# Unequal halves for the products of the values in a two-layer linear-attention kernel

## The chip, the cores and the metric

The kernel runs on one core of a Trainium2 chip, as one program. The metric is the time of the device in microseconds (us), the median of several runs. One further run was taken with the hardware profiler; what is said of single engines comes from that one.

## What is computed

A stack of four residual blocks on 2048 rows of 640 numbers: attention, a dense block, then the same two again with the same weights. Cut to what matters here:

```python
qkv = (x @ wqkv).reshape(B, S, 3, H, Dh)            # H = 32 heads of Dh = 20
q, k, v = qkv[0], qkv[1], qkv[2]                    # after a transpose, per head
phi_q = concat([softmax(q @ w_phi), softmax(-(q @ w_phi))])
phi_k = concat([softmax(k @ w_phi), softmax(-(k @ w_phi))])
kv = einsum("bhsf,bhsd->bhfd", phi_k, v)
z = phi_k.sum(axis=s)
o = (phi_q @ kv) / (phi_q @ z + 1e-6)
x = x + o.reshape(B, S, D) @ wo                     # D = 640; x is normed before
x = x + mish(norm(x) @ w1 + b1) @ w2                # F = 1536
```

The change concerns `v`: for every row, 640 sums of products (32 heads times 20) from a normed row of 640.

## The kernel before

The 2048 rows are 16 tiles of 128, taken two by two in 8 blocks. Per layer there are three parts: `attend_first` makes queries, keys and values of each tile and adds up `kv` and `z` over all tiles; `attend_second` turns them into the attention's output; `dense` is the dense block. Each part runs over the 8 blocks. Both layers do the same, so that values are made for 32 tiles in all.

**Split numbers.** Every product with weights is done three times in the reduced-precision format `F32R`, on high and low parts (`h` and `l`): high rows with high weights, high with low, low with high. `project_half` (L352 to L359) does this for the values, the keys, the queries and the output projection: for each of five chunks k of 128 input columns it issues three TensorE products, so 15 for one half of the output columns. All have the line L358 in the profile. The stationary operand of each is a 128x128 piece of the rows (`xth` or `xtl`), which is loaded anew by a weight load before each product (PEld in the profile); the moving operand is a piece of the weights, `w` columns wide. `project` (L343) calls it for both halves. For the values `w` is HC = 320, for keys and queries FC = 304 (19 differences per head).

**Values.** `values` (L448) makes one tile: a column of ones, 30 products of 320 columns in two halves, and a copy by ScalarE out of PSUM into the tile `v`, where each head has 21 columns. In the first block of a layer (i < BT, 2 tiles) the halves go to two one-bank PSUM tiles `one` and are copied one by one; in the other blocks (14 tiles per layer) they go to the two banks of one tile `mm`, and one instruction copies all 640 columns. There are two `mm` buffers, which keys, queries, values and the output projection share.

**Order.** For TensorE, VectorE and GpSimd a scheduler decides the order when the program is built. ScalarE's copies and activations go through the helper `act` (L116; in the profile they all have the line L122), which ties each to the one before, so that they keep the order of the code. `keys` and `queries` are generators that are taken on step by step; their features (`features`, L374) are a copy out of `mm`, reductions and differences on VectorE, an exponential on ScalarE, a sum and a quotient, and for queries a transpose and a store to `e_d`. Each block works its tiles in an order of its own, in most of them k0, v0, q0, k1, v1, q1. The product of keys and values (L432) reads the finished `v`. A query's tile `r` is one of two buffers, and ScalarE's first write to it waits until the store of the tile before last has left.

Of the kernel before, what the change touches and what calls it, by code (L numbers as in the profile page):

```python
# [10 lines left out]
AF = mybir.ActivationFunctionType  # L11
# [7 lines left out]
D = 640  # L19
F = 1536  # L20
H = 32
DH = 20
KD = D // P
KF = F // P
BT = 2
# [4 lines left out]
HC = D // 2  # L30
# [18 lines left out]
def kernel(  # L49
# [22 lines left out]
    def mm_tile():  # L72
        return psum.tile([P, 2, 512], F32, tag="mm", name="mm", bufs=2)

    def one_tile():
        return psum.tile([P, 512], F32, tag="one", name="one", bufs=4)
# [39 lines left out]
    def act(*args, **kw):  # L116

        if last_act[0] is None:
            ins = nc.scalar.activation(*args, **kw)
        else:  # L120
            with tc.issue_after(last_act[0]):
                ins = nc.scalar.activation(*args, **kw)  # L122
        last_act[0] = ins.ins
# [49 lines left out]
    def load_v_weights():  # L173

        ws = [r1_pair(k) for k in range(KD)]
        for k in range(KD):
            split(ws[k][0][:, D:2 * D], ws[k][1][:, D:2 * D], wv[k * P:(k + 1) * P, :],
                  (row_tile, row_tile, v_tile, v_tile, big_tile)[k])
        return ws
# [163 lines left out]
    def project(xts, t, ws, col, ps=None, w=HC):  # L343

        if ps is None:
            mm = mm_tile()
            ps = [mm[:, 0], mm[:, 1], mm]
        for c in range(2):
            project_half(ps[c], xts, t, ws, col, c, w=w)
        return ps  # L350

    def project_half(ps, xts, t, ws, col, c, ks=range(KD), w=HC):  # L352
        sl = slice(t * P, (t + 1) * P)
        cs = slice(col + c * w, col + (c + 1) * w)
        for k in ks:
            h, l, wh, wl = xts.hs[k], xts.ls[k], ws[k][0][:, cs], ws[k][1][:, cs]
            for n, (a, r) in enumerate(((h, wh), (h, wl), (l, wh))):
                nc.tensor.matmul(ps[:, :w], a[:, sl], r, start=(k == 0 and n == 0),  # L358
                                 stop=(k == KD - 1 and n == 2))  # L359

    def both(ps, w=HC):

        return ps[2][:, :, :w]
# [43 lines left out]
    def attend_first(layer, x_src, first):  # L407
# [40 lines left out]
        def values(xts, i, v):  # L448
            vv = v.rearrange("p (h d) -> p h d", d=DH + 1)
            act(vv[:, :, DH], ident[:, :H], AF.Copy, scale=0.0, bias=1.0)  # L450
            if i < BT:
                pv = project(xts, i, kv_ws, D, [one_tile(), one_tile()])
                for c in range(2):
                    act(vv[:, c * H // 2:(c + 1) * H // 2, :DH],
                        pv[c][:, :HC].rearrange("p (h d) -> p h d", d=DH), AF.Copy)
            else:
                pv = project(xts, i % BT, kv_ws, D)
                act(vv[:, :, :DH].rearrange("p (c h) d -> p c h d", c=2),
                    both(pv).rearrange("p c (h d) -> p c h d", d=DH), AF.Copy)
            yield  # L460

        if first is None:
            with tc.manual_schedule(engines={mybir.EngineType.SP}):
# [11 lines left out]
                kv_ws = load_v_weights()  # L475
# [3 lines left out]
        else:  # L479
            nxt, kv_ws = first  # L480
            q_ws = load_q_weights()
        for b in range(NB):
            xts = nxt
# [8 lines left out]
            for n, (kind, t) in enumerate(order):  # L492
                t = int(t)
                i = b * BT + t
                if b == 0 and n == 1:
                    if layer:
                        load_k_weights(kv_ws)
                if b == 0 and n == 3:
                    if layer == 0:
                        fold_phi(kv_ws, bd, raw)  # L500
                    kva = one_tile()
                if b == NB - 1 and n == 3:
                    loaded = {0: load(0)}
                if b + 1 < NB:
                    if n == 0:
                        xt = fetch_normed(b + 1)
                    elif n == 2:
                        nxt = xt if layer else normed(b + 1, xt)
                    elif n > 2:
                        nxt.step()  # L510
                g = {"k": lambda: keys(xts, i, vs[t]), "q": lambda: queries(xts, i),
                     "v": lambda: values(xts, i, vs[t])}[kind]()
                next(g)
                advance()
                pending.append(g)
# [388 lines left out]
```

## Time and profile before

| what | us |
|---|---|
| median of 3 runs (lowest to highest) | 1399.29 (1398.11 to 1399.91) |
| the profiled execution's own time | 1397.5 |
| its span in the profile | 1395.7 |
| TensorE busy | 1364.8 |
| weight loads busy | 1344.2 |
| VectorE busy | 1080.8 |
| ScalarE busy | 592.4 |
| GpSimd busy | 466.4 |

The span reaches from the first to the last instruction; the 1.8 us that the time has beyond it lie around the program. PE is TensorE's matmul, PEld its weight load, DVE is VectorE, ACT ScalarE, POOL GpSimd. A matmul's duration in the profile is its latency, and the next starts long before it ends: what a product costs in a stream is the distance from one start to the next, which the timeline shows. Each matmul has its own weight load.

### The profile page before, as it was taken

The numbers are of one execution on the slowest core, as the hardware profiler recorded it, in microseconds if no ns is written. First come the engines' busy times: TensorE is split into PE (matmuls) and PEld (weight loads), VectorE is DVE, ScalarE is ACT, GpSimd is POOL, SyncE is SP. The second block draws the span as 40 slices with busy tenths as digits, with TensorE's granted clock in tenths as the row PEclk, the third lists the DMA queues.
The fourth block names the chain that finished last, engine by engine and source line by source line (L and its number), as shares of the span: only waits on it lengthen the run. The fifth ranks groups of instructions, "written<-read, shape, count | busy, mean of one in ns | idle before, by whom it ended". The sixth has DMA issues, their size and how long they took to land. (4 is left out here: it accounts for less than half of the span.)

```text
span 1395.7 us, 30855 instructions
## 1 busy us (share of the span) xinstructions
PE 1364.8 (98%) x12866; PEld 1344.2 (96%) x12866; DVE 1080.8 (77%) x1814; ACT 592.4 (42%) x1039; POOL 466.4 (33%) x346
## 2 busy tenths in 40 slices
PE   7999999999999999999999999999999999999998
PEld 7989999899999999999999999999999999999998
DVE  5798888686688877788759988878667766777775
ACT  4444443321355454454454334332134544444443
POOL 1454544243442221222234454543344211211112
PEclk9999999999999999999999999999999999999999
DMA  8533423779534433444374333358965212333200
GB/s 312 166 60 77 75 41 70 204 224 317 194 89 95 100 82 60 102 114 95 103 258 85 78 72 70 58 126 253 273 246 172 76 29 68 95 96 95 59 37 20
DMA packets 350277, 169.03 MB, mean 121 GB/s; under 512 B 287097, under 2 KB 323689, under 8 KB 350137
## 3 DMA queue, kind: packets, MB, share of 16 engines
q1 hardware_dynamic: 350137, 167.06, 44.4%
q8 instruction: 101, 1.65, 0.5%
q14 instruction: 39, 0.32, 0.1%
HBM read 104.43 MB, written 62.59 MB: 120 GB/s over the span
## 5 line engine op out<-in xcount | busy, mean ns | idle before, releaser
L745 PE MATMUL mm<-r2h,ol 128*128 128x320 f32 x1280 | 305.3, 310 | 1.4 <-ACT ol L728 0.8
L729 POOL TENSOR_TENSOR ol<-big,ol 128x512 fp32r<-128x512 f32 (+1 forms) x98 | 130.1, 1329 | 456.2 <-ACT ol L728 390.9
L703 PE MATMUL one<-xtl,r1h 128*128 128x256 f32 x960 | 268.6, 280 | 2.0 <-DVE xtl L300 2.0
L703 PE MATMUL one<-xth,r1l 128*128 128x256 f32 x960 | 268.0, 279 | 0.0
L703 PE MATMUL one<-xth,r1h 128*128 128x256 f32 x960 | 266.5, 279 | 0.0
L745 PEld LDWEIGHTS mm<-r2h,ol 128*128 128x128 f32 x1280 | 219.1, 188 | 2.7 <-POOL ol L729 1.5
L745 PE MATMUL mm<-r2l,ol 128*128 128x320 f32 x640 | 197.3, 309 | 0.0
L358 PE MATMUL mm<-r1h,xth 128*128 128x304 f32 (+1 forms) x600 | 187.5, 313 | 6.6 <-ACT r L122 6.6
L358 PE MATMUL mm<-r1h,xtl 128*128 128x304 f32 (+1 forms) x600 | 184.7, 308 | 1.0 <-DVE xtl L300 1.0
L358 PE MATMUL mm<-r1l,xth 128*128 128x304 f32 (+1 forms) x600 | 184.4, 307 | 0.0
L703 PEld LDWEIGHTS one<-xtl,r1h 128*128 128x128 f32 x960 | 180.4, 188 | 2.7 <-DVE xtl L300 2.5
L703 PEld LDWEIGHTS one<-xth,r1l 128*128 128x128 f32 x960 | 180.4, 188 | 0.0
L703 PEld LDWEIGHTS one<-xth,r1h 128*128 128x128 f32 x960 | 179.9, 188 | 0.0
L718 DVE TENSOR_SCALAR big<-big 128x512 f32<-128x512 f32 (+1 forms) x98 | 55.9, 571 | 113.6 <-ACT big L716 113.5
L358 PE MATMUL mm<-r2h,xth 128*128 128x304 f32 (+1 forms) x460 | 142.2, 309 | 0.0
L358 PE MATMUL mm<-r2h,xtl 128*128 128x304 f32 (+1 forms) x460 | 140.4, 305 | 0.0
L358 PE MATMUL mm<-r2l,xth 128*128 128x304 f32 (+1 forms) x460 | 140.3, 305 | 0.0
L716 ACT ACTIVATE big<-one,b1s 128x256 f32<-128x256 f32 x192 | 80.8, 469 | 96.2 <-PE one L703 95.6
L358 PEld LDWEIGHTS mm<-r1h,xth 128*128 128x128 f32 x600 | 113.8, 190 | 8.1 <-ACT r L122 7.0
L720 ACT ACTIVATE big<-big,two 128x512 f32<-128x512 f32 (+1 forms) x98 | 70.3, 717 | 118.8 <-DVE big L719 116.2
L745 PEld LDWEIGHTS mm<-r2l,ol 128*128 128x128 f32 x640 | 120.2, 188 | 0.0
L399 POOL TENSOR_TENSOR r<-r,r 128x1280 f32<-128x1280 f32 x32 | 77.0, 2406 | 124.1 <-DVE r L398 108.7
(131 smaller groups left out, 3031.9 us busy)
## 6 DMA issues: line engine op xcount, KB each, us to landing
e_d<-r SPq DMA_DIRECT2D x128, 160.0 KB, 4.0
big<-e_d SPq DMA_DIRECT2D x32, 640.0 KB, 5.9
x_d<-xt SPq DMA_DIRECT2D x23, 640.0 KB, 3.9
xt<-x_d SPq DMA_DIRECT2D x22, 640.0 KB, 4.6
n_d<-xn SPq DMA_DIRECT2D x176, 80.0 KB, 2.3
xt<-in_x SPq DMA_DIRECT2D x16, 640.0 KB, 5.5
xn<-x_d SPq DMA_DIRECT2D x28, 320.0 KB, 4.1
v<-n_d SPq DMA_DIRECT2D x30, 256.0 KB, 3.1
```

The lines of the kernel that those rows point to most:

```text
L358: nc.tensor.matmul(ps[:, :w], a[:, sl], r, start=(k == 0 and n == 0), stop=(k == KD - 1 and n == 2))
L399: nc.gpsimd.tensor_tensor(eg, eg, r.unsqueeze(2).to_broadcast([P, 2 * H, DH]), op=ALU.mult)
L703: nc.tensor.matmul(ph[:, j, :], l, r, start=(n == 0), stop=(n == 3 * KD - 1))
L716: exps[0] = nc.scalar.activation(part(ta, 0)[:, j - js.start], ph[:, j, :], AF.Exp, bias=b1s[:, 2 * pr + j:2 * pr + j + 1]).ins
L718: nc.vector.tensor_scalar_min(e, e, E_CAP)
L720: nc.scalar.activation(r, n, AF.Ln, bias=two)
L729: nc.gpsimd.tensor_tensor(al[:, js], n, ah[:, js].bitcast(F32), op=ALU.subtract)
L745: nc.tensor.matmul(pys[t][:, c, :HC], l[:, j, sl], r, start=(f == 0 and n == 0), stop=(f == KF - 1 and n == 2))
```

## The change

The halves of the values become 24 heads (480 columns) and 8 heads (160 columns). The 24 heads go to the first PSUM bank, the 8 to the second. Each part is copied by an instruction of its own, in all blocks, and the first copy stands in ScalarE's order ahead of the second. The number of products and of weight loads stays: 15 of 480 and 15 of 160 columns in place of 30 of 320.

```diff
             if i < BT:
-                pv = project(xts, i, kv_ws, D, [one_tile(), one_tile()])
-                for c in range(2):
-                    act(vv[:, c * H // 2:(c + 1) * H // 2, :DH],
-                        pv[c][:, :HC].rearrange("p (h d) -> p h d", d=DH), AF.Copy)
+                pv = [one_tile(), one_tile()]
             else:
-                pv = project(xts, i % BT, kv_ws, D)
-                act(vv[:, :, :DH].rearrange("p (c h) d -> p c h d", c=2),
-                    both(pv).rearrange("p c (h d) -> p c h d", d=DH), AF.Copy)
+                mm = mm_tile()
+                pv = [mm[:, 0], mm[:, 1]]
+            for c, (h0, h1) in enumerate(((0, 24), (24, H))):
+                n = (h1 - h0) * DH
+                project_half(pv[c], xts, i % BT, kv_ws, D + h0 * DH - c * n, c, w=n)
+                act(vv[:, h0:h1, :DH], pv[c][:, :n].rearrange("p (h d) -> p h d", d=DH), AF.Copy)
             yield
```

`project_half` takes the columns from `col + c * w`; for c = 1 the argument `D + 480 - 160` makes that D + 480.

## The prediction

> **What bounds the kernel now.** I read the page's first part for the busiest engine, then the busy time of stretches that hold the values (75 to 255 us and, in the second layer, 740 to 935 us), then TensorE's waits, and then the groups of products by shape and the timeline for what one product costs. The first part and four of the stretches:
>
> ```profile
> PE 1364.8 (98%) x12866; PEld 1344.2 (96%) x12866; DVE 1080.8 (77%) x1814; ACT 592.4 (42%) x1039; POOL 466.4 (33%) x346
> ```
>
> ```profile
> 75.00:100.00 25.00, 21.52 (x256) 20.58 (x256) 24.97 (x31) 9.07 (x15) 15.44 (x9) 0.93 0.28 53
> ...
> 150.00:200.00 50.00, 50.00 (x562) 49.22 (x549) 43.84 (x57) 22.59 (x38) 26.52 (x15) 1.00 0.32 58
> ...
> 740.00:780.00 40.00, 35.84 (x414) 34.79 (x413) 39.56 (x40) 14.82 (x25) 20.46 (x10) 0.96 0.33 71
> ...
> 830.00:880.00 50.00, 50.00 (x568) 49.22 (x554) 43.44 (x49) 19.88 (x34) 25.23 (x12) 1.00 0.38 71
> ```
>
> The columns are length, PE, PEld, DVE, ACT, POOL, TensorE's granted clock and the DMA. TensorE works 98% of the span and every microsecond of the steady stretches, at clock 1.00. Only early in each layer has it gaps (3.5 us before 100, 4.2 us before 780), and there VectorE is full. The waits say what for:
>
> ```profile
> PE mm L358 <- ACT r L122: 6.6, 2, 3.5
> ```
>
> That is one stall per layer (3.5 and 3.1 us): both `mm` buffers are taken, and ScalarE's copy of a query comes late. Outside of these, time added to TensorE's stream is time added to the end.
>
> **What one product costs.** The products of the values, 960 in all (840 into `mm`, 120 into `one`):
>
> ```profile
> L358 PE MATMUL mm<-r1h,xth 128*128 128x320 f32 x280 | 88.2, 315 | 3.1 <-ACT r L122 3.1
> L358 PE MATMUL mm<-r1h,xtl 128*128 128x320 f32 x280 | 87.2, 311 | 0.0
> L358 PE MATMUL mm<-r1l,xth 128*128 128x320 f32 x280 | 87.1, 311 | 0.0
> ...
> L358 PE MATMUL one<-r1h,xtl 128*128 128x320 f32 x40 | 12.3, 309 | 0.0
> L358 PE MATMUL one<-r1l,xth 128*128 128x320 f32 x40 | 12.3, 309 | 0.0
> ...
> L358 PE MATMUL one<-r1h,xth 128*128 128x320 f32 x40 | 11.5, 312 | 0.0
> ```
>
> A duration of 0.31 us is latency. The distance of starts is read from the timeline, first and last row of an unbroken run, for three widths:
>
> ```profile
> 199.83 0.31 PE L358 MATMUL mm<-r1h,xtl 128*128 128x320 f32 x1
> ...
> 202.03 0.31 PE L358 MATMUL mm<-r1h,xtl 128*128 128x320 f32 x1
> ...
> 202.53 0.30 PE L358 MATMUL mm<-r2l,xth 128*128 128x304 f32 x1
> ...
> 206.45 0.30 PE L358 MATMUL mm<-r2h,xtl 128*128 128x304 f32 x1
> ```
>
> ```profile
> 385.83 0.28 PE L703 MATMUL one<-xth,r1h 128*128 128x256 f32 x1
> ...
> 390.03 0.28 PE L703 MATMUL one<-xth,r1h 128*128 128x256 f32 x1
> ```
>
> 320 columns: 15 steps in 2.20 us, 0.1467 each. 304 columns: 28 steps in 3.92 us, 0.1400. 256 columns: 36 steps in 4.20 us, 0.1167. From 304 to 320 a column costs 0.42 ns (0.0067/16), from 256 to 320 it costs 0.47 (0.0300/64).
>
> **480 columns** aren't in the trace. By the nearer slope: 0.1467 + 160 x 0.00042 = 0.2133 us; by the wider: 0.1467 + 160 x 0.00047 = 0.2217. I take 0.2133, since the rows next to it give it.
>
> **160 columns** aren't in the trace in this format. If cost followed the columns down by the same 0.42 ns, it would be 0.0800, and the pair would cost what two halves cost: nothing gained, nothing lost. What speaks against that is the weight load, one per product, 128 columns wide whatever the moving operand is. Two views: the loads after a pause, and the narrow products of L250 (float32, two instructions per product).
>
> ```profile
> 164.45 0.19 PEld L358 LDWEIGHTS mm<-r1h,xth 128*128 128x128 f32 x1
> 164.56 0.19 PEld L358 LDWEIGHTS mm<-r1l,xth 128*128 128x128 f32 x1
> 164.71 0.19 PEld L358 LDWEIGHTS mm<-r1h,xtl 128*128 128x128 f32 x1
> ```
>
> ```profile
> 38.73 1.28 PE L250 MATMUL one<-big,raw 120*128 120x114 f32 x10
> 39.94 0.41 PE L250 MATMUL one<-big,r 40*128 40x38 f32 x2
> ```
>
> ```profile
> L250 PE MATMUL one<-big,raw x17: 275/275/365, 37.7 to 40.7; 120*128 120x114 f32 x17
> ...
> L250 PE MATMUL one<-big,r x4: 277/288/298, 39.9 to 41.0; 40*128 40x38 f32 x4
> ```
>
> The second load follows the first by 0.11 us, when the queue has room; the third comes 0.15 later, as a product must first start. So loads hardly follow closer than 0.11, and one load at a time runs ahead. Ten products of 114 columns stand (1.28 - 0.275)/9 = 0.1117 us apart, and two of 38 columns 0.41 - 0.288 = 0.12: a third of the columns and not a nanosecond less. That is a floor, set by loads of 128 columns. I take 0.112 for 160 columns (nearest below in width, 114); the ends are 0.11 (the loads) and 0.1167 (256 columns, which 160 can't exceed by width).
>
> The Trainium skill ("TensorE: Matmul & The Clock Gate", LDWEIGHTS) puts a load at its columns over 1.2, which is 107 ns for 128, and the sum would then be 13.0 us in place of the 15.4 below. The same page (Back-to-back issue gap) has streams of load and product at about 81 ns for 128 columns and 131 for 512, which by a straight line between them makes 480 and 160 together as dear as twice 320: no change. The trace has 0.1117 for 114 columns and 0.1467 for 320, so that it speaks for the first.
>
> **The sum.** 480 pairs (32 tiles x 15). A pair before: 2 x 0.1467 = 0.2933. After: 0.2133 + 0.112 = 0.3253. Difference 0.032, times 480: **+15.4 us**. Ends: 480 x (0.2133 + 0.11 - 0.2933) = 14.4, and 480 x (0.2217 + 0.1167 - 0.2933) = 21.6.
>
> **The copies.** ScalarE's rows, and what it waits for ahead of writing `v`:
>
> ```profile
> L122 ACT ACTIVATE v<-mm 128x640 f32<-128x640 f32 x28 | 19.8, 707 | 78.8 <-PE mm L358 78.8
> ...
> L122 ACT ACTIVATE v<-one 128x320 f32<-128x320 f32 x8 | 3.2, 432 | 4.9 <-PE one L358 4.9
> ```
>
> A column costs (707 - 432)/320 = 0.86 ns, so 480 columns take 570 ns and 160 take 295: 865 in place of 707 in 28 tiles, 4.4 us more on an engine that is busy 42%; in the other four nothing changes (2 x 432 = 864). TensorE's stream hides it.
>
> **A new wait.** The order of the changed program shows that in those 28 tiles the first 160-column product waits for ScalarE's copy of the 480 columns, as both lie in one tile `mm`; before, the second half followed at once. The scheduler put other work between: 22 to 25 products of the next query in most tiles, 22 x 0.140 = 3.1 us, and 1.6 us in the shortest (the last block of the second layer). The copy needs 0.57 us. Is ScalarE there in time? Before the 28 copies it idled 78.8 us, 2.8 per tile, until both halves were done, 30 x 0.1467 = 4.4 us after the start. The first part is done at 15 x 0.2133 = 3.2, 1.2 us sooner, so ScalarE has 1.6 us in hand and the cover another 2.5. I cost the wait at nothing; without the cover it would be 0.57 us in each of 28 tiles, 16 us.
>
> Behind the second copy ScalarE now stands still until the 160 columns are done, and the exponential of the query before is queued there. One half block of before:
>
> ```profile
> 159.21 0.71 ACT L122 ACTIVATE v<-mm 128x640 f32<-128x640 f32 x1 [3.56 <-PE mm L358]
> 159.82 1.26 ACT L122 ACTIVATE r<-r 128x1280 f32<-128x1280 f32 x1
> ...
> 163.41 0.68 ACT L122 ACTIVATE r<-mm 128x608 f32<-128x608 f32 x1 [0.55 <-PE mm L358]
> ...
> 168.97 0.69 ACT L122 ACTIVATE big<-mm 128x608 f32<-128x608 f32 x1 [3.07 <-PE mm L358]
> ```
>
> Counted from the end of the keys (154.8), the exponential starts at 5.0 now. In the new order the keys' second half and the 480 columns are interleaved; then come 0.21 us of 480 columns, 22 products (3.1) and 15 x 0.112 = 1.7, so the copy of the 160 starts at about 5.2 (latency counted) and the exponential at 5.5. The query's copy starts at 8.6 now and at 8.65 then, since the same work of TensorE lies ahead of it. Both `mm` buffers come free in time: the values' at 5.5 (needed at 7.3, after 8 products and L432), the query's at 9.3 (needed at about 12). So the half blocks stay bound by TensorE and become 0.48 us longer each.
>
> **At the two stalls** TensorE waits for a chain on ScalarE, VectorE and DMA that doesn't get longer. Up to 3.5 tiles of values come before each, 1.7 us per layer that can vanish in it; but the new order leaves one group of 160 columns (15 x 0.112 = 1.7) for after the stall in the first layer. I take 1 us off for both layers (bounds: 3.4 off, and 1.7 on per layer).
>
> Sum: +15.4 - 1 = +14.4. On the profiled execution, 1397.5 + 14.4 = 1411.9; the median of the runs lies 1.8 above that execution, so **1413.7 us**.
>
> **The rivals.**
> 1. *No floor* (the other side): the load of a narrow product hides under the wide ones, the distance falls to 0.080, and the time stays at 1399, within 2 us either way; where the shorter last copy (295 for 707 ns) also frees `mm` early enough, it eats from the two stalls (6.6 us) and the kernel gets a little faster. It decides as soon as a load can stand more than one product ahead. The 0.12 of 38 columns speaks against it, and the Back-to-back gap that the Trainium skill states speaks for it.
> 2. *The new wait shows.* If ScalarE comes to the first copy more than 2.5 us after the 480 columns are done, TensorE stands before the 160 with the rest of the query and the next keys queued behind. One exponential late (1.26 us) would cost about 1 us in each of 28 tiles: 1413.7 + 28 = 1442. For it: ScalarE does wait for VectorE and stores early in each layer. Against it: 2.8 us of idle time per tile.
> 3. *160 columns cost what float32 costs.* No product under 256 columns in this format is in the trace. The float32 products of L250 need two instructions each, 2 x 0.1117 for 114 columns, and by columns 0.314 for 160: 480 x (0.2133 + 0.314 - 0.2933) = +112, 1511 us. Nothing in the trace asks for it; it is the upper end of what is unknown.
>
> That the change doesn't do what it says is out: the order has 480 products of each width, and the same loads.
>
> **How the numbers follow.** Forecast 0.72, rival 1 0.08, rival 2 0.12, rival 3 0.06, others 0.02. The forecast's own bounds are 1399.3 + 14.4 - 3.4 = 1410 and 1399.3 + 21.6 + 3.4 = 1424. For 8 in 10 the range must take in most of rival 2 where it shows in part of the tiles, up to 1432, and a forecast some us lower where the narrow products gain a little on the floor, 1405. A run of this kernel tells about 0.2% (2.8 us) from no change. Slower takes the forecast, rivals 2 and 3 and half of the others: 0.91; rival 1 splits into 0.06 the same and 0.03 faster.
>
> **What would show it.** In the changed profile's timeline the 160-column products would stand 0.11 us apart and the 480-column ones 0.213; TensorE stays at 50.00 of 50.00 in the steady stretches; the waits name no copy of `v` for more than a microsecond or two in all; the half blocks are 0.5 us longer. Wrong I am if the 160s stand 0.08 apart (rival 1), 0.2 or more (rival 3), or if TensorE's gaps grow with ScalarE's copy of `v` as their end (rival 2).

## The result and the profile after

The changed kernel takes 1434.63 us (median of 4 runs, 1434.15 to 1436.97), the kernel before beside it 1399.60 (1398.11 to 1402.36): a ratio of 1.0257, 95% interval 1.0238 to 1.0276. That is 35 us slower, where 14 were forecast. The profiled execution has a span of 1432.6 us, 36.9 more than before.

First the products. The changed kernel's timeline, from the second to the last product of one group of each width:

```profile
146.71 0.38 PE L358 MATMUL mm<-r1l,xth 128*128 128x480 f32 x1
...
149.56 0.38 PE L358 MATMUL mm<-r1h,xtl 128*128 128x480 f32 x1
...
153.29 0.28 PE L358 MATMUL mm<-r1l,xth 128*128 128x160 f32 x1
...
154.75 0.27 PE L358 MATMUL mm<-r1h,xtl 128*128 128x160 f32 x1
```

13 steps each: 480 columns cost 2.85/13 = 0.219 us, 160 columns 1.46/13 = 0.112. So the floor is there, at the price that was forecast; the wide product costs 0.219 in place of 0.2133. A pair is 0.038 us dearer than before, 18 us for 480 pairs. That leaves half of the loss.

Then the first part of the page and the stretches of the changed kernel (length, PE, PEld, DVE, ACT, POOL, clock, DMA):

```profile
PE 1387.7 (97%) x12866; PEld 1348.8 (94%) x12866; DVE 1088.0 (76%) x1814; ACT 592.4 (41%) x1067; POOL 463.1 (32%) x346
```

```profile
150.00:200.00 50.00, 48.89 (x508) 46.09 (x507) 42.45 (x60) 17.96 (x34) 25.28 (x16) 1.00 0.34 61
...
830.00:880.00 50.00, 47.35 (x495) 44.81 (x495) 40.27 (x44) 17.21 (x32) 19.38 (x10) 1.00 0.33 62
```

TensorE, full there before, now has gaps of 1.1 and 2.7 us in 50. ScalarE's busy time is as before (592.4). TensorE's waits:

```profile
PE one L432 <- POOL big L399: 12.8, 4, 5.5
PE mm L358 <- ACT r L122: 11.3, 6, 4.3
...
PE mm L358 <- ACT big L122: 2.8, 5, 0.6
```

The first and the last row are new, and the middle one was 6.6 with two cases. In return a wait at the end of the first part is gone that the kernel before had:

```profile
PE one L564 <- DVE xn L558: 5.3, 2, 2.7
```

By these rows the waits have grown by 12.8 + 4.7 + 2.8 - 5.3 = 15 us. With the 18 of the products that is 33 of the 36.9. A wait also costs more than its row says, 0.34 us in the case taken apart in the last section; for 11 waits more that would be about 4, an estimate from that one case.

No row names a copy of `v`: TensorE never waits long for the copy that the change puts between its two groups. It waits for a product of GpSimd that follows an exponential, for the copy of a query, and for the copy of the keys. The first two come behind the copies of `v` in ScalarE's order; the keys' copy comes ahead of them. The waits of ScalarE show where the first two were held:

```profile
ACT v L122 <- PE mm L358: 150.5, 45, 4.6
```

Before `v` it now idles 150.5 us, where it was 78.8. One half block of the changed kernel:

```profile
164.30 0.68 ACT L122 ACTIVATE big<-mm 128x608 f32<-128x608 f32 x1 [5.50 <-PE mm L358]
164.87 0.26 ACT L122 ACTIVATE v<-ident 128x32 f32<-128x32 f32 x1
164.99 0.57 ACT L122 ACTIVATE v<-mm 128x480 f32<-128x480 f32 x1
170.04 0.30 ACT L122 ACTIVATE v<-mm 128x160 f32<-128x160 f32 x1 [4.48 <-PE mm L358]
170.24 1.26 ACT L122 ACTIVATE r<-r 128x1280 f32<-128x1280 f32 x1
```

After the copy of the 480 columns ScalarE stands still for 4.48 us, until TensorE has done 22 query products and the 160 columns, and only then comes to the exponential. Here that passes. It does not pass in two places. One is the end of the first part of the attention, where too few query products are left to fill the time. The chain of what ended last, around 272 us:

```profile
268.32 4.59 PE mm L358 x36
...
272.94 0.02 ACT v L122
...
273.14 1.27 ACT big L122
...
274.43 1.49 DVE r L397
...
276.78 1.28 POOL r L389
```

and GpSimd's rows there:

```profile
276.78 1.27 POOL L389 TENSOR_TENSOR r<-r,m 128x640 f32<-128x640 f32 x1 [3.85 <-DVE m L388]
278.01 2.35 POOL L399 TENSOR_TENSOR big<-big,r 128x1280 f32<-128x1280 f32 x1
```

The exponential of the last keys stands behind the copy of the last 160 columns. It runs at 273.14, the sum on VectorE at 274.43, and GpSimd's product, in order behind the query's difference, ends at 280.4. TensorE's product of keys and values waits for it 5.5 us. In the kernel before, 45 query products stood between the last values and that product (254.28 to 260.44), and the same exponential ran at their start:

```profile
254.47 0.71 ACT L122 ACTIVATE v<-mm 128x640 f32<-128x640 f32 x1 [3.34 <-PE mm L358]
255.08 1.26 ACT L122 ACTIVATE big<-big 128x1280 f32<-128x1280 f32 x1
```

The other place is the second layer. There the exponential of a query, held in the same way, leaves VectorE idle for 2.90 us; later ScalarE stands still until the store of an earlier query has left, so that its copy of the next query comes late and TensorE waits for it:

```profile
835.82 1.49 DVE L397 TENSOR_REDUCE r<-r 128x64 f32<-128x1280 f32 x1 [2.90 <-ACT r L122]
...
854.45 0.26 ACT L122 ACTIVATE r<-ident 128x32 f32<-128x32 f32 x1 [3.66 <-DMA e_d<-r]
854.59 0.66 ACT L122 ACTIVATE r<-mm 128x608 f32<-128x608 f32 x1
...
855.30 0.49 PE L358 MATMUL mm<-r1h,xth 128*128 128x480 f32 x1 [2.65 <-ACT r L122]
```

The kernel before has no wait of TensorE for a query's copy after 760 us.

### The profile page after: what moved, and what is told of

Read it like the earlier page. It is cut to its first block, busy times and chain, and to the rows that moved or that the text cites. A ratio compares the mean times of both kernels' runs of the same rounds, so it can differ in the third digit from the quotient of the medians.

```text
span 1432.6 us, 30914 instructions
## 1 busy us (share of the span) xinstructions
PE 1387.7 (97%) x12866; PEld 1348.8 (94%) x12866; DVE 1088.0 (76%) x1814; ACT 592.4 (41%) x1067; POOL 463.1 (32%) x346
## 4 chain that ended last, share of the span: by engine, by line
PE 75%; DVE 11%; DMA 3%; issue 2%; ACT 2%; SPq 1%; POOL 0%; DVEq 0%; ACTq 0%; POOLq 0%
PE one L703 22%; PE mm L745 21%; PE mm L358 20%; PE one L358 6%; PE mm L594 3%; DMA e_d<-r 2%; DVE m L388 2%; DVE r L397 2%; PE one L294 2%; DVE xtl L300 1%; SPq L444 1%; PE one L432 1%; DVE r L440 1%; DVE big L718 1%; DVE r L391 1%
## 5 line engine op out<-in xcount | busy, mean ns | idle before, releaser
L358 PE MATMUL mm<-r1h,xth 128*128 128x304 f32 (+2 forms) x600 | 192.4, 321 | 11.3 <-ACT r L122 11.3
L358 PE MATMUL mm<-r1l,xth 128*128 128x304 f32 (+2 forms) x600 | 189.6, 316 | 0.0
L358 PE MATMUL mm<-r1h,xtl 128*128 128x304 f32 (+2 forms) x600 | 188.8, 317 | 0.0
L358 PE MATMUL mm<-r2h,xth 128*128 128x304 f32 (+1 forms) x460 | 143.0, 311 | 2.8 <-ACT big L122 2.8
L358 PE MATMUL mm<-r2l,xth 128*128 128x304 f32 (+1 forms) x460 | 140.9, 306 | 0.0
L358 PE MATMUL mm<-r2h,xtl 128*128 128x304 f32 (+1 forms) x460 | 140.8, 306 | 0.0
L358 PEld LDWEIGHTS mm<-r1h,xth 128*128 128x128 f32 x600 | 114.3, 191 | 18.0 <-ACT r L122 12.9
L358 PEld LDWEIGHTS mm<-r1h,xtl 128*128 128x128 f32 x600 | 113.9, 191 | 4.3
```

## The experiments

Theory A says that two things add up: products of 160 columns at the floor of the weight load, and ScalarE held in order at the second copy. Its rivals were that the widths alone did it, that the second copy's own time did it, and later that the products (a second group that comes late, a PSUM buffer held longer) and not ScalarE's order did it. Ratios are to runs of the kernel before on the same chip. All variants are edits of the changed kernel's `values`, if nothing else is said.

**Both groups of products ahead of both copies** (24 and 8 heads).

The calls' arguments are cut:

```diff
-            for c, (h0, h1) in enumerate(((0, 24), (24, H))):
-                n = (h1 - h0) * DH
+            parts = [(c, h0, h1, (h1 - h0) * DH) for c, (h0, h1) in enumerate(((0, 24), (24, H)))]
+            for c, h0, h1, n in parts:
                 project_half(...)
+            for c, h0, h1, n in parts:
                 act(...)
```

> 24 and 8 heads as in the changed kernel, but both groups of products stand ahead of both copies, so that no product waits for a copy within a tile. Theory A (two causes: narrow products at the floor of the weight load, 480 x (0.220 + 0.112 - 0.2933) = 18.6 us, and the wait between copy and second group, which holds ScalarE, about 17 us): about 1399.5 + 18.6 = 1418, with TensorE full again in the steady stretches and no wait of L432 for GpSimd. Rival B (all of the loss comes from the widths, as they upset the order): stays at 1434. Rival C (the second copy's own time on ScalarE, 4.4 us, does it): about 1430.

Measured 1413.51 us, 1.0093 (1.0080 to 1.0107), 4.5 us less than the 1418 expected. TensorE is full again in the steady stretches, as its windows show:

```profile
150.00:200.00 50.00, 50.00 (x576) 47.68 (x575) 40.86 (x55) 23.26 (x42) 24.76 (x15) 1.00 0.31 55
830.00:880.00 50.00, 50.00 (x510) 47.53 (x509) 43.61 (x50) 17.91 (x35) 22.37 (x11) 1.00 0.43 79
```

A block of two tiles, from one copy of ones to that of the next block, takes on ScalarE's timeline:

```profile
159.74 0.26 ACT L122 ACTIVATE v<-ident 128x32 f32<-128x32 f32 x1
...
189.37 0.26 ACT L122 ACTIVATE v<-ident 128x32 f32<-128x32 f32 x1
```

29.63 us. In the kernel before it is 28.57, in the changed one 30.54:

```profile
155.40 0.25 ACT L122 ACTIVATE v<-ident 128x32 f32<-128x32 f32 x1
...
183.97 0.25 ACT L122 ACTIVATE v<-ident 128x32 f32<-128x32 f32 x1
```

```profile
164.87 0.26 ACT L122 ACTIVATE v<-ident 128x32 f32<-128x32 f32 x1
...
195.41 0.26 ACT L122 ACTIVATE v<-ident 128x32 f32<-128x32 f32 x1
```

So the widths cost 0.53 us a tile, 17 us over 32 tiles; a block of the second layer gives the same (28.57 against 27.50 us). The profiled executions differ by 1411.9 - 1395.7 = 16.2 us, the runs by 13 (11 to 15); TensorE's wait for ScalarE's copy of the query is 5.3 us here, 6.6 before. The other 0.9 us a block, and the waits at the end of the first part and in the second layer, go with the order of the copies. Rivals B and C are out.

Where the loss lies can be read from the timelines, by the first product of L358 with which the attention's output projection begins (`one<-r2h,xth` with 320 columns: 276.22 and 951.75 before, 292.80 and 988.58 in the changed kernel, 284.96 and 967.92 here) and by the second layer's first product of values (712.00, 728.54 and 720.70). More than the kernel before, in us:

| stretch | changed kernel | products first |
|---|---|---|
| up to the first layer's output projection | 16.6 | 8.7 |
| values to output projection, second layer | 20.3 | 7.5 |
| all the rest | 0.0 | 0.0 |

So the order of the copies costs 7.9 us in the first layer and 12.8 in the second.

**Equal halves with a copy between** (`((0, 16), (16, H))` in place of `((0, 24), (24, H))`).

> Equal halves of 320 columns as before, but the first is copied ahead of the second group's products, as in the changed kernel. Theory A: no cost of products (the 320s stay at 0.1467), only the wait: about 1399.5 + 16 = 1416, with gaps of TensorE at the end of each attention's first part, ended by GpSimd's product of the last keys. Rival B (widths alone): 1399.5. Rival C (second copy's own time): about 1404.

Measured 1429.67, 1.0212 (1.0198 to 1.0226): the order alone, with no narrow product, costs 29 us, more than the 16 expected. TensorE's first two waits are those of the changed kernel, the first of them larger:

```profile
PE mm L358 <- ACT r L122: 16.9, 6, 6.0
PE one L432 <- POOL big L399: 13.1, 5, 6.0
```

The two causes do not simply add (13 + 29 is more than 35). In the steady blocks of the first layer they do: a block takes 29.51 us, 0.9 more than the 28.57 before, and with 24 and 8 heads the order costs the same 0.9.

```profile
162.06 0.26 ACT L122 ACTIVATE v<-ident 128x32 f32<-128x32 f32 x1
...
191.57 0.26 ACT L122 ACTIVATE v<-ident 128x32 f32<-128x32 f32 x1
```

In the second layer they do not: from the first product of values to the output projection it is 21.8 us longer than before (723.54 to 985.07), though no product is dearer, where the changed kernel's order costs 12.8. ScalarE waits longer for the stores of queries there, 39.5 us after 700 us against 27.9 in the changed kernel. Why it does isn't shown; the second group is longer here (15 x 0.1467 = 2.2 us for 1.7), but ScalarE's idle time before `v` is the same (151.0 and 150.5 us).

**Equal halves, products first, two copies.**

> Equal halves of 320 columns, both groups of products first, then two copies of 320 in place of one of 640. Theory A: the copies cost ScalarE 28 x (2 x 432 - 707) = 4.4 us, which TensorE hides: 1399.5, within 2 us. Rival C (the copies' time is on the path): 1404 or more.

Measured 1400.45, 1.0000 (0.9990 to 1.0010). A second copy of its own costs nothing.

**22 and 10 heads and 20 and 12 heads, products first** (440 and 200, 400 and 240 columns).

> 22 and 10 heads, 440 and 200 columns, products first. If a column costs 0.458 ns with no fixed part and 0.112 us is the floor, a pair costs 0.2017 + 0.112 = 0.3137 in place of 0.2933, 480 x 0.0203 = 9.8 us: about 1409. If there is no floor at a width but a fixed extra cost for any narrow product (the step at 160 is a property of 160 to 256), it could be anything from 1399.5 to 1418.

> 20 and 12 heads, 400 and 240 columns, products first. By 0.458 ns a column and a floor of 0.112 us: 240 columns cost 0.112 in place of 0.110, the pair 0.2952 in place of 0.2933, 480 x 0.002 = 1 us: 1400 to 1402. If the floor reached up to 256 columns at 0.117, 480 x 0.007 = 3.4 us: 1404.

Measured 1406.92, 1.0044 (1.0028 to 1.0061), and 1400.38, 1.0008 (0.9998 to 1.0018). The narrow products of the first, on the timeline:

```profile
174.45 0.27 PE L358 MATMUL mm<-r1l,xth 128*128 128x200 f32 x1
...
175.90 0.28 PE L358 MATMUL mm<-r1h,xtl 128*128 128x200 f32 x1
```

1.45/13 = 0.1115: 200 columns cost what 160 cost. With 240 it is 1.47/13 = 0.113:

```profile
171.72 0.27 PE L358 MATMUL mm<-r1l,xth 128*128 128x240 f32 x1
...
173.19 0.27 PE L358 MATMUL mm<-r1h,xtl 128*128 128x240 f32 x1
```

That is hardly above the 0.110 that 0.458 ns a column would give, and the loss is within the noise. The 10 us forecast for 22 heads came out as 6, again less in the runs than by the products.

**The second copy behind the exponential** (24 and 8 heads; the generator stops ahead of it, and the loop takes it on once the other generators have moved; the code is cut).

```diff
                 project_half(...)
+                if c:
+                    yield
                 act(...)
...
                 next(g)
                 advance()
+                if kind == "v":
+                    next(g)
                 pending.append(g)
```

> The changed kernel, with one thing moved: in ScalarE's order the copy of the 160 columns stands behind the exponential of the query (or key) before, not ahead of it. The 160-column products still wait for the first copy, with other products between. Theory A1 (the loss beyond the widths comes from ScalarE standing still at the second copy, with the exponential queued behind it): most of the 21 us go, 1414 to 1419, and TensorE's wait for GpSimd's product of the last keys is gone. Rival A2 (it comes from the products: the second group late, and the values' buffer held for 8.6 us in place of 5.1): stays above 1428.

Measured 1420.64, 1.0158 (1.0143 to 1.0174): 14 of the 21 us between 1434.6 and 1413.5 are gone, somewhat fewer than expected (1414 to 1419). At the end of the first part ScalarE's rows are now:

```profile
263.66 0.57 ACT L122 ACTIVATE v<-mm 128x480 f32<-128x480 f32 x1 [3.21 <-PE mm L358]
264.13 1.27 ACT L122 ACTIVATE big<-big 128x1280 f32<-128x1280 f32 x1
268.80 0.30 ACT L122 ACTIVATE v<-mm 128x160 f32<-128x160 f32 x1 [3.40 <-PE mm L358]
```

The exponential runs 4.7 us ahead of the copy that held it, and no wait of L432 for GpSimd is left among TensorE's waits. So the larger part of the second cause hangs on where the copy stands in ScalarE's order (A1). That ScalarE's standing still is the whole of it isn't shown: the scheduler answered with another order of TensorE as well, in which the 480 columns no longer run in between the keys' products, and the wait for the keys' copy is gone too.

Some 7 us stay that the products-first kernel doesn't have. They don't lie in the steady blocks (29.71 us against 29.63). TensorE's wait for the query's copy at the early stalls has 2.6 of them (7.9 us, against 5.3), and the wait ahead of L564's transposes (here a few lines on) 0.9. Whether the values' buffer, held longer, makes the 2.6 (A2) is open: equal halves with the products first have 7.9 in that row too. The rest I could not assign.

**A PSUM tile for each half.** 24 and 8 heads, then equal halves, in the changed order, with `pv = [one_tile(), one_tile()]` in all blocks.

> 24 and 8 heads in the changed order (product, copy, product, copy), but in all blocks the halves lie in two PSUM tiles of one bank each, so that no product waits for a copy of the same tile; keys and queries have the mm buffers to themselves. Theory A: the widths' 13 us stay and the wait's 21 us go: 1413, or some us less, as the early stalls of both layers (6.6 us, both mm buffers taken) may shrink. If the order of the copies alone costs time, 1425 or more.

> Equal halves of 320 columns in two one-bank tiles in all blocks, each copied by itself. Theory A: no floor, no shared tile: 1400 or up to 6 us less, if the early stalls shrink. If holding ScalarE at the second copy matters though the tiles are apart (the scheduler still puts queries between the halves), slower: 1405 to 1420.

Measured 1406.20, 1.0048 (1.0033 to 1.0062), and 1402.02, 1.0019 (1.0007 to 1.0030). With 24 and 8 heads the wait is gone, and with it the early stalls; of TensorE's wait for ScalarE's copy of a query 0.2 us is left. The longest waits are now:

```profile
PE mm L250 <- DMA raw<-in_wqk_t: 6.0, 2, 4.3
PE one L561 <- DVE xn L555: 4.9, 2, 2.6
PE mm L250 <- DVE big L236: 3.1, 1, 3.1
PE one L700 <- DVE xtl L300: 2.0, 2, 1.0
```

A block takes 29.67 us (155.60 to 185.27 by the copies of ones), what it takes with the products first (29.63). So the order product, copy, product, copy need not cost anything, and what it costs in the changed kernel goes with both halves lying in one tile `mm`. The run changes two things at once, though: no product waits for a copy of its own tile, and the values leave both `mm` buffers to the keys and queries; which of them counts for how much isn't shown. With equal halves the scheduler finds another order, with waits for VectorE's `xtl` (4.3 us) and GpSimd's product (4.1 us) in place of the stalls, and nothing is won.

**The kernel before with two one-bank tiles in the first three or two blocks** (`if i < 3 * BT`, `if i < 2 * BT` with `project(xts, i % BT, ...)`).

> The kernel before, with its two one-bank tiles for the values not only in the first block of a layer but in the first three; later blocks as before (halves of 320, one copy). Theory A: the early stalls of both layers (6.6 us and what follows them), where both mm buffers are taken, go, and nothing else changes: 1393 to 1397. Rival: the stalls come from VectorE, which is full there, and only move: 1400.

> The same with the first two blocks of a layer. The stall before the third block's keys had the second block's values in one mm buffer; with these elsewhere it goes: 1393 to 1397, and the order from the third block on is that of the kernel before. Rival (VectorE's bound, stall only moves): 1400.

Measured 1399.03, 0.9997 (0.9987 to 1.0007), and 1397.81, 0.9985 (0.9974 to 0.9997). The 1393 to 1397 of theory A was missed both times; the rival's 1400 is nearer. The early stalls, 6.6 us of TensorE's waits, are gone in both, and the time falls by 0.4 and 1.6 us: most of it comes back elsewhere, 4.1 and 4.7 us of it in a wait of L432 for GpSimd's product that the kernel before does not have. I found no version that is clearly faster than the kernel before.

## Why the prediction was wrong

The direction was right, and the range's upper end was 2.6 us short. The step that failed is "I cost the wait at nothing": the order of the copies, in one tile, cost about 21 us. Point by point:

- *The floor* (160 columns at 0.112): right, 0.112 measured, and the same for 200 columns. Rivals 1 and 3 are out, and so are the streams of the Trainium skill ("TensorE: Matmul & The Clock Gate", Back-to-back issue gap): against its 131 ns for 512 columns stand 219 for 480.
- *480 columns at 0.2133*: 0.219. The distances per column are 0.1167/256 = 0.456, 0.1400/304 = 0.461, 0.1467/320 = 0.458 and 0.219/480 = 0.457 ns: simply proportional. My slope of 0.42 between 304 and 320 took a difference of 0.0067 us out of rows printed to 0.01; dividing by the whole width would have given 0.220. The term was 15.4 and measures 17 to 18.
- *The copies* hidden by TensorE: right (1.0000 with two copies).
- *The stalls take 1 us off*: 5.3 for 6.6 us of waits where the second wait is absent. That it agrees may be luck, since the same row has 7.9 with equal halves and the products first.
- *"I cost the wait at nothing"* failed. TensorE indeed hardly waits for the first copy, as I argued; but I priced the wait by the instruction that waits and not by ScalarE, which stands still for 4.5 us at the second copy in most of the tiles. I did follow that, for one steady half block alone, and there I was nearly right: the exponential came 5.9 us after the copy of the keys began (164.30 to 170.24), against 5.5 forecast and 5.0 before. I did not follow it to the end of the part, where the filler runs out and the last keys' exponential, sum and product come after it in a row (5.5 us of wait in the first layer), nor to the second layer, where the query's store, and with it ScalarE's next query, came late (12.8 us in all in that layer).
- *"Both mm buffers come free in time"*: I asked when the values' and the query's buffers were needed again, but not the keys'. Where the keys and the 480 columns are interleaved, the values keep their buffer, and the query's first product waits for the keys' copy: 2.8 us in 5 cases. "So the half blocks stay bound by TensorE and become 0.48 us longer each" held with the products first (0.53), not in the changed kernel (0.98).
- *Rival 2* had the right price in size (28 us, measured about 21), but the wrong place: it had ScalarE late at the first copy. ScalarE was early there and late behind the second. Its sign, gaps that end with a copy of `v`, did not show, and "the waits name no copy of `v`" came true in a kernel 21 us slower than forecast: as a sign it watched the wrong instruction.
- *The number of the products-first kernel*, 1413.5, is the forecast's 1413.7, and that is partly luck: the widths' term was 2 to 3 us too small, and the runs show about 4 us less than the steady blocks give.

In sum: 17 for the widths by the steady blocks, 13 as the runs show them; and about 21 for the second copy's place in ScalarE's order and the shared tile, for which I had nothing.

## What to carry to other kernels

A product whose columns take less time than its weight load gains nothing from being narrower (here below about 245 columns); before splitting unequally, look for the narrowest products in the trace and see whether their distance still follows the width. When a reader is put between two writers of one tile, follow the reader's whole engine: what stands behind it in order, at the end of the stage as well as in the middle, where the scheduler has no more work to put between. Take a price per column by dividing a long run by the whole width, rather than from the difference of two near widths.

## What the runs showed of the hardware

- Products in `F32R` with a weight load of 128 columns each cost the larger of 0.457 ns a column (256 to 480 columns) and about 0.112 us (160, 200 and 240 columns), without a fixed part that I could see; 0.112/0.457 puts the place where the two meet at about 245 columns. That the load sets the floor is argued, not shown by a run of its own. For it: instructions as such can follow closer, since the 64 products of L432 for one tile, with a load of 21 columns each, take 0.83 us (171.08 in the changed kernel); but these are written to different strips of partitions, so it is a hint only.
- A PSUM wait of 0.55 us costs TensorE more than itself: with the order of copies between, a block was 0.9 us longer (30.54 against 29.63), and the one wait inside it (at 165.03) had 0.55 us in the timeline. The same wait one block earlier:

```profile
133.42 0.52 PE L358 MATMUL mm<-r1h,xtl 128*128 128x304 f32 x2
134.49 0.41 PE L358 MATMUL mm<-r2h,xth 128*128 128x304 f32 x1 [0.55 <-ACT big L122]
134.73 0.30 PE L358 MATMUL mm<-r2l,xth 128*128 128x304 f32 x1
```

The first row covers products at 133.42 and, a step of 0.14 later, at 133.56; the next starts at 134.49. So 0.93 us lie between two starts that would be 0.14 apart: the pause shows as idle only once the latency of the last product is over. The product after it follows 0.24 later in place of 0.14. Together that is 0.89 us lost, 0.34 more than the row says, and just what the block is longer.
